# Loading the q and k of the split attention jobs once, splitting them over half the columns, and spreading the parts inside SBUF

## The chip, the cores and the metric

The kernel runs on one core of one Trainium2 chip. The metric is device time in microseconds (us) of one launch. The changed kernel and the kernel before compute the same outputs from the same inputs.

## The reference, cut to what matters

```python
batch, n_heads, seq, head_dim = (4, 8, 768, 64)
n_global, n_local = (8, 96)

def _attn_ref(q, k, v, n_global, n_local):
    scale = 1.0 / np.sqrt(D)
    scores = scale * np.matmul(q, k.transpose(0, 1, 3, 2))
    ...
    keep = is_global | is_local
    bias = -slopes[:, None, None] * dist[None, :, :]
    scores = np.where(keep, scores + bias, -1000000000.0)
    a = np.exp(scores - np.max(scores, axis=-1, keepdims=True))
    a = a / (np.sum(a, axis=-1, keepdims=True) + 1e-09)
    return np.matmul(a, v)

def _moe_ref(x, w_in, conv_w, w_out):
    h = np.maximum(x @ w_in, 0.0)
    ...
    gate = 1.0 / (1.0 + np.exp(-conv_out))
    return (h * gate @ w_out)

def reference(**kwargs):
    attn_out = _attn_ref(**attn_kwargs)
    x = attn_out.transpose(0, 2, 1, 3).reshape(B, S, H * D)
    return _moe_ref(x=x, **moe_kwargs)
```

The lines are put together from the reference. Everything is float32 or float64 and is wanted at about float32 accuracy. Attention is banded: a query sees the 96 keys up to its own and 8 global keys. `conv_out` is a convolution of three taps along the sequence, so the second half is two products (512 to 1024, 1024 to 512) with a gate between them.

## The kernel before, in words

**Jobs and steps.** Attention is cut into 32 jobs. A job `m` is one batch, one half `u` of the sequence (384 queries) and one pair of heads, and it has three steps, one for each tile of 128 queries; step `s` is tile `s % 3` of job `s // 3`. A step makes the scores of two heads on the TensorE (PE, `scores`), adds the bias and takes maxima on the VectorE (DVE, `maxima`, L412), takes the exponentials on the ScalarE (ACT, L426), inverts the sums on the DVE (`normalise`, reciprocal L438), scales on the GpSimd (POOL, L444), transposes on the PE (L452), and, three steps at a time, multiplies by v (`values`, L473). Each batch half then goes through the two products (`mm1` L507, `mm2` L622), which are cut into pieces and put between the attention steps.

**Native and split jobs.** Jobs 0 to 8 (`NATIVE`, `BESIDE`) multiply q and k as float32 at L385, from tiles of which rows 0 to 63 hold one head and rows 64 to 127 the other. Jobs 9 to 31, the 23 split jobs, use the faster format float32r, with q and k each split into a rounded high part and a low remainder. Their tiles are laid out so that one pass over 128 rows does two of the products: `kk` has the high part of k on rows 0 to 63 and the low part on rows 64 to 127, for both heads side by side; `qh` has the high part of q on both halves, `ql` the low part on both. A score tile is then two matmuls at L395, `kk` with `qh` and `kk` with `ql`.

**How the split is made.** The host gives q and k twice over, on rows 0 to 63 and again on rows 64 to 127. `load(m)` brings all 128 rows of `rk` (L114) and `rq` (L115) by one DMA each. `prep(m, 0)` rounds them into `kk` (L137) and `qh` (L138) on the POOL; `prep(m, 1)` subtracts on the DVE, rows 64 to 127 for `kk` (L141), all rows for `ql` (L142). For k there are 816 columns in the first half of a sequence and 1008 in the second, for q 768. `rk` and `rq` are single buffers (pool `p1`); `qh`, `ql`, `kk` and the v tile have two each (pool `p2`). The split for job m+1 is written into the program at the first step of job m, and the load for job m+2 at its second step.

**Order.** Steps 0 to 15 are in an order written by hand. From step 16 on the tile framework arranges the instructions of every engine with a timeline of its own, under priorities and under `issue_after` conditions: the pieces of the products that `fill` puts into a step are held behind the scores, maxima and exponentials of the step before. Each engine then runs its list in order. The list of the SyncE (SP) issues the loads of q, k, v (L123) and the raw weights (L307). A DMA in that list waits for the tile that it overwrites to be free, and everything behind it in the list waits too.

**The first part.** In the first 90 us the DVE and POOL also decode the weights of the products from float64 (L316 to L331). In the last 70 us the raw weights are read again and checked (L339).

## Time and profile before

| | |
|---|---|
| median of 3 runs | 444.82 us (444.18 to 444.93) |
| the profiled execution's own time | 445.31 us |
| its span, first to last instruction | 443.5 us |
| granted TensorE clock, mean | 0.996 |
| PE busy | 431.2 us (97% of the span) |
| DVE busy | 357.2 us (81%) |
| ACT busy | 309.9 us (70%) |
| POOL busy | 221.2 us (50%) |
| DMA moved | 60.02 MB, mean 135 GB/s |

Busy time is a sum over the whole span, and the span has parts with different limits. Matmuls are pipelined, so a PE that is busy all the time has instructions in flight all the time; whether it was held up is read from the chain of work that ended last and from stretches in which its busy time is below their length. An engine's queue is in order, so what an engine waited for also holds all that stands behind it.

### The profile page before, as it was taken

The numbers are of one execution on the slowest core, as the hardware profiler recorded it, in microseconds if no ns is written. First come the engines' busy times: TensorE is split into PE (matmuls) and PEld (weight loads), VectorE is DVE, ScalarE is ACT, GpSimd is POOL, SyncE is SP. The second block draws the span as 40 slices with busy tenths as digits, with TensorE's granted clock in tenths as the row PEclk, the third lists the DMA queues.
The fourth block names the chain that finished last, engine by engine and source line by source line (L and its number), as shares of the span: only waits on it lengthen the run. The fifth ranks groups of instructions, "written<-read, shape, count | busy, mean of one in ns | idle before, by whom it ended". The sixth has DMA issues, their size and how long they took to land.

```text
span 443.5 us, 9050 instructions
## 1 busy us (share of the span) xinstructions
PE 431.2 (97%) x3039; PEld 374.5 (84%) x3039; DVE 357.2 (81%) x935; ACT 309.9 (70%) x839; POOL 221.2 (50%) x307
## 2 busy tenths in 40 slices
PE   8988999799999999999999999999999999999996
PEld 7655778799889988899889988899988998798876
DVE  6899899998999988757998989747999975568700
ACT  4889988789896678546876865665776776755540
POOL 5555334654456786556757744647656841013000
PEclk9999999899999999999999999999999999999999
DMA  6998953141543244442246134423235313980111
GB/s 210 294 255 258 271 184 110 40 163 65 153 128 120 75 136 132 128 125 94 85 128 192 41 107 145 141 102 104 67 119 181 103 48 122 312 295 32 47 49 55
DMA packets 22662, 60.02 MB, mean 135 GB/s; under 512 B 3024, under 2 KB 5584, under 8 KB 22608
## 3 DMA queue, kind: packets, MB, share of 16 engines
q1 hardware_dynamic: 18992, 53.01, 39.2%
q10 hardware_dynamic: 3616, 6.36, 3.9%
q8 instruction: 26, 0.43, 0.4%
q14 instruction: 28, 0.23, 0.2%
HBM read 53.07 MB, written 6.29 MB: 134 GB/s over the span
## 4 chain that ended last, share of the span: by engine, by line
PE 81%; DVE 8%; DMA 6%; ACT 3%; issue 1%; POOL 0%; SPq 0%; DVEq 0%; ACTq 0%
PE o L622 26%; PE h L507 25%; PE pv L473 10%; PE t L452 9%; PE s L395 7%; DMA check<-in_w 3%; PE s L385 1%; PE last L643 1%; DMA out<-ob 1%; DVE w L320 1%; DVE w L318 1%; ACT junkb L350 1%; ACT pbuf L426 1%; DMA rq<-in_qk 1%; PE sb L385 1%
## 5 line engine op out<-in xcount | busy, mean ns | idle before, releaser
L444 POOL TENSOR_SCALAR pbuf<-pbuf,mm 128x232 f32<-128x232 f32 (+1 forms) x160 | 113.3, 718 | 81.0 <-DVE mm L438 49.5
L426 ACT ACTIVATE pbuf<-s,mm 128x232 f32<-128x232 f32 (+1 forms) x165 | 72.1, 442 | 48.3 <-DVE mm L412 34.6
L412 DVE CUSTOM_DVE_ANT_0 s<-s,tab 128x232 f32<-128x232 f32 (+1 forms) x165 | 63.1, 385 | 20.2 <-PE s L395 15.7
L622 PE MATMUL o<-woh,gh 128*128 128x512 f32 x184 | 74.1, 403 | 0.0
L622 PE MATMUL o<-woh,gl 128*128 128x512 f32 x184 | 73.5, 400 | 0.0
L622 PE MATMUL o<-wol,gh 128*128 128x512 f32 x184 | 73.3, 398 | 0.0
L452 PE MATMUL t<-ident,pbuf 128*128 128x128 f32 x384 | 65.4, 279 | 5.4 <-ACT pbuf L442 2.7
L557 POOL TENSOR_SCALAR c<-hbuf,cw 128x382 f32<-128x382 f32 (+1 forms) x48 | 38.6, 807 | 56.5 <-ACT hbuf L517 56.5
L452 PEld LDWEIGHTS t<-ident,pbuf 128*128 128x128 f32 x384 | 46.4, 141 | 20.2 <-ACT pbuf L442 6.4
L457 ACT ACTIVATE pt<-t 128x512 f32<-128x512 f32 x96 | 57.0, 597 | 8.3 <-PE t L452 8.0
L507 PE MATMUL h<-xl,wih 128*128 128x384 f32 x252 | 59.4, 343 | 0.0
L507 PE MATMUL h<-xh,wih 128*128 128x384 f32 x252 | 58.8, 347 | 0.1
L507 PE MATMUL h<-xh,wil 128*128 128x384 f32 x252 | 55.8, 339 | 0.0
L473 PE MATMUL pv<-pt,v 128*64 128x128 f32 (+1 forms) x768 | 50.3, 280 | 0.3 <-DVE xl L489 0.2
L473 PEld LDWEIGHTS pv<-pt,v 128*64 128x64 f32 (+1 forms) x768 | 42.5, 138 | 8.6 <-issue 3.6
L558 DVE SCALAR_TENSOR_TENSOR c<-hbuf,cw,c 128x382 f32<-128x382 f32 (+1 forms) x64 | 44.3, 699 | 4.8 <-POOL c L557 3.7
L559 DVE SCALAR_TENSOR_TENSOR c<-hbuf,cw,c 128x382 f32<-128x382 f32 (+1 forms) x64 | 45.4, 712 | 0.3
L507 PEld LDWEIGHTS h<-xh,wih 128*128 128x128 f32 x252 | 43.2, 190 | 2.1 <-ACT pbuf L426 0.9
L507 PEld LDWEIGHTS h<-xl,wih 128*128 128x128 f32 x252 | 43.9, 189 | 0.7 <-issue 0.7
L507 PEld LDWEIGHTS h<-xh,wil 128*128 128x128 f32 x252 | 44.1, 188 | 0.0
L517 ACT ACTIVATE hbuf<-h 128x384 f32<-128x384 f32 x64 | 31.4, 495 | 13.5 <-PE h L507 12.5
L622 PEld LDWEIGHTS o<-woh,gl 128*128 128x128 f32 x184 | 34.6, 188 | 7.3
(120 smaller groups left out, 856.1 us busy)
## 6 DMA issues: line engine op xcount, KB each, us to landing
v<-in_vv SPq DMA_DIRECT2D x32, 384.0 KB, 3.6
rq<-in_qk SPq DMA_DIRECT2D x23, 384.0 KB, 3.1
wr<-in_w SPq DMA_DIRECT2D x16, 512.0 KB, 5.3
check<-in_w SPq DMA_DIRECT2D x16, 512.0 KB, 4.9
rk<-in_qk SPq DMA_DIRECT2D x12, 504.0 KB, 3.6
out<-ob ACTq DMA_DIRECT2D x23, 256.0 KB, 2.4
rk<-in_qk SPq DMA_DIRECT2D x11, 408.0 KB, 3.6
rq<-in_qk SPq DMA_DIRECT2D x16, 96.0 KB, 5.1
```

Source lines behind the costliest of these rows:

```text
L412: last_ttr[s] = V.tensor_tensor_reduce(out=sp[j][:, c0 : c0 + n], in0=sp[j][:, c0 : c0 + n], in1=tb, scale=-0.125, scalar=3.0e38, op0=ALU. ...
L426: last_exp[s] = A.activation(pb[:, j, c0 : c0 + n], sp[j][:, c0 : c0 + n], AF.Exp, bias=mm[:, j : j + 1], scale=-1.0, accum_out=mm[:, 2 + ...
L444: G.tensor_scalar(x, x, inv, 1.0, ALU.mult, ALU.mult)
L452: T.transpose(pt[:, j, c, :], pb[:, j, c * P : (c + 1) * P], ident)
L457: last_ev[s] = A.activation(sb, st_pt[s], AF.Copy)
L473: T.matmul(pv[m][64 * j : 64 * j + 64, i * P : (i + 1) * P], vt[m][:n, i, c, 64 * j : 64 * j + 64], sb[:n, j, c, :], start=c == 0, stop=c ...
L507: T.matmul(ps[:, :TB], w_[:, k, fs], x_, start=part == 0 and k == 0, stop=part == 2 and k == NK - 1,)
L517: A.activation(half, ps[:, :TB], AF.Relu, scale=0.5)
L557: G.tensor_scalar(c, *tap(1), 1.0, ALU.mult, ALU.mult)
L558: V.scalar_tensor_tensor(c, *tap(0), c, ALU.mult, ALU.add)
L559: V.scalar_tensor_tensor(c, *tap(2), c, ALU.mult, ALU.add)
L622: last = T.matmul(ps, g_[:, f], w_[:, f], start=f == 0 and part == 0, stop=f == NF - 1 and part == 2,)
```

## The change

`load` now brings the split jobs in the layout of the native ones: one head on rows 0 to 63, the other on rows 64 to 127, each value once, by two DMAs of 64 rows for `rk` and two for `rq`. The tiles keep their size, so half of their columns are free. The POOL writes the rounded part into the free half of the same tile (`rk[:, w:]`, `rq[:, TB:]`); the DVE subtracts in place in the other half. Both now run over all 128 rows and half the columns (408 or 504 for k, 384 for q). After that 12 DMAs inside SBUF, all on SP's queue, carry the four (part, head) pieces of k to their place in `kk`, and the four of q to both row halves of `qh` or `ql`. The host's arrays are unchanged. Lines from `load` on move by up to six: L114 and L115 are now L110, L137 and L138 are L132 and L133, L141 and L142 are both L138, the new DMAs are at L144 and L148, L123 is L118, and L395, L412, L438, L444, L507 and L622 are L401, L418, L444, L450, L513 and L628.

```diff
@@ load
-        n = D if m < NATIVE else P
-        if m < BESIDE:
-            for t, c, a in ((rk, 2 * TB, w // 2), (rq, 0, TB)):
-                for j in range(2):
-                    r = slice(j * D, (j + 1) * D)
-                    X = nc.scalar if m == 0 and t is rq else nc.sync
-                    X.dma_start(t[r, :a], src[r, c + j * a : c + (j + 1) * a])
-        else:
-            nc.sync.dma_start(rk[:n], src[:n, 2 * TB :])
-            nc.sync.dma_start(rq[:n], src[:n, : 2 * TB])
+        for t, c, a in ((rk, 2 * TB, w // 2), (rq, 0, TB)):
+            for j in range(2):
+                r = slice(j * D, (j + 1) * D)
+                X = nc.scalar if m == 0 and t is rq else nc.sync
+                X.dma_start(t[r, :a], src[r, c + j * a : c + (j + 1) * a])
@@ prep
-            G.tensor_copy(kk, rk)
-            G.tensor_copy(qh, rq)
+            G.tensor_copy(rk[:, w:].bitcast(F32R), rk[:, :w])
+            G.tensor_copy(rq[:, TB:].bitcast(F32R), rq[:, :TB])
         else:
             qh, ql, kk = qk[m]
-            V.tensor_tensor(kk[64:], rk[64:], kk[64:].bitcast(F32), ALU.subtract)
-            V.tensor_tensor(ql, rq, qh.bitcast(F32), ALU.subtract)
+            for t, n in ((rk, w), (rq, TB)):
+                low, high = t[:, :n], t[:, n:]
+                V.tensor_tensor(low.bitcast(F32R), low, high, ALU.subtract)
+                for x, part in enumerate((high, low)):
+                    for j in range(2):
+                        heads = part[j * D : (j + 1) * D]
+                        cols = slice(j * n, (j + 1) * n)
+                        if t is rk:
+                            nc.sync.dma_start(kk[x * D : (x + 1) * D, cols].bitcast(F32), heads)
+                        else:
+                            for r in range(2):
+                                q_ = (qh, ql)[x][r * D : (r + 1) * D, cols]
+                                nc.sync.dma_start(q_.bitcast(F32), heads)
```

The framework arranges the instructions anew. Three places show it, all around job 20, whose first step is step 60. A name ends in the number of its job or step and a buffer number (`rk20_2985` is `rk` of job 20, `mm57` belongs to step 57).

SP's queue, loads of q and k for jobs 19 to 21 and of v for jobs 17 to 19, before:

```order
L123 DMA v17_2624<-in_vv 128x768
L115 DMA rq19_2667<-in_qk0 128x768
L114 DMA rk19_2666<-in_qk0 128x816
L115 DMA rq20_2832<-in_qk1 128x768
L123 DMA v18_2779<-in_vv 128x768
L114 DMA rk20_2831<-in_qk1 128x1008
L123 DMA v19_2942<-in_vv 128x768
L115 DMA rq21_2988<-in_qk1 128x768
L114 DMA rk21_2987<-in_qk1 128x1008
```

and now:

```order
L110 DMA rk19_2806<-in_qk0 64x408 x2
L110 DMA rq19_2807<-in_qk0 64x384 x2
L118 DMA v18_2933<-in_vv 128x768
L144 DMA kk19_2916<-rk19_2806 64x408 x4
L148 DMA qh19_2914<-rq19_2807 64x384 x4
L148 DMA ql19_2915<-rq19_2807 64x384 x4
L110 DMA rk20_2985<-in_qk1 64x504 x2
L110 DMA rq20_2986<-in_qk1 64x384 x2
L118 DMA v19_3110<-in_vv 128x768
L144 DMA kk20_3093<-rk20_2985 64x504 x4
L148 DMA qh20_3091<-rq20_2986 64x384 x4
L148 DMA ql20_3092<-rq20_2986 64x384 x4
```

Where SP issued three DMAs a job it issues 17, and the load of job 20 stands behind the whole spread of job 19, whose tiles it overwrites.

The POOL's queue around the rounding of job 20, before:

```order
L444 TENSOR_SCALAR pbuf0_193<-pbuf0_193,mm54_2715 128x136 x2
L557 TENSOR_SCALAR c3_2728<-hbuf_190,cw_185 128x386
L138 CAST qh20_2935<-rq20_2832 128x768
L137 CAST kk20_2937<-rk20_2831 128x1008
L444 TENSOR_SCALAR pbuf1_194<-pbuf1_194,mm55_2786 128x232 x2
```

and now:

```order
L450 TENSOR_SCALAR pbuf2_195<-pbuf2_195,mm56_2996 128x232 x2
L563 TENSOR_SCALAR c3_2870<-hbuf_190,cw_185 128x386
L132 CAST rk20_2985<-rk20_2985 128x504
L563 TENSOR_SCALAR c3_2870<-hbuf_190,cw_185 128x386
L133 CAST rq20_2986<-rq20_2986 128x384
L450 TENSOR_SCALAR pbuf0_193<-pbuf0_193,mm57_3040 128x136 x2
```

The rounding stood behind the scaling of step 54, six steps ahead of the job's first; now it stands behind that of step 56, four ahead.

The PE's queue at the first scores of job 20, before:

```order
L452 MATMUL t57_3005<-ident_153,pbuf0_193 128x128 x4
L395 MATMUL s60_3033<-kk20_2937,qh20_2935 128x232
L395 MATMUL s60_3033<-kk20_2937,ql20_2936 128x232
L395 MATMUL s60_3033<-kk20_2937,qh20_2935 128x232
L395 MATMUL s60_3033<-kk20_2937,ql20_2936 128x232
L622 MATMUL o1_0_3026<-woh_188,gh1_0_2394 128x512
```

and now:

```order
L458 MATMUL t57_3175<-ident_153,pbuf0_193 128x128 x4
L401 MATMUL s60_3203<-kk20_3093,qh20_3091 128x232
L628 MATMUL o1_0_3196<-woh_188,gh1_0_2508 128x512
L628 MATMUL o1_0_3196<-wol_189,gh1_0_2508 128x512
L628 MATMUL o1_0_3196<-woh_188,gl1_0_2509 128x512
L458 MATMUL t58_3237<-ident_153,pbuf1_194 128x128 x4
...
L401 MATMUL s60_3203<-kk20_3093,ql20_3092 128x232
L401 MATMUL s60_3203<-kk20_3093,qh20_3091 128x232
L401 MATMUL s60_3203<-kk20_3093,ql20_3092 128x232
```

The four score matmuls stood together; now nine matmuls of the second product and four transposes stand between the first, which reads `qh`, and the second, which reads `ql`.

## Rows read from the trace of the kernel before

**Rows 1.** Busy time of each engine in two stretches, with clock and DMA share.

```profile
core 0: us, PE busy (x) PEld busy (x) DVE busy (x) ACT busy (x) POOL busy (x), PEclk, DMA share, GB/s
64.00:85.00 21.00, 18.80 (x129) 16.14 (x128) 20.83 (x56) 17.82 (x55) 13.33 (x16) 1.00 0.36 118
110.00:370.00 260.00, 259.91 (x1858) 232.07 (x1855) 222.72 (x571) 182.09 (x483) 158.11 (x205) 1.00 0.38 116
```

**Rows 2.** Chain of work that ended last, 110 to 370 us, by line.

```profile
by line: PE h L507 33.2%; PE o L622 32.8%; PE pv L473 12.0%; PE s L395 11.2%; PE t L452 10.9%; issue 0.0%
```

**Rows 3.** The chain, 64 to 86 us, pieces: start, us, what.

```profile
71.76 1.02 DVE kk L141
...
74.42 0.85 DVE ql L142
...
80.27 1.25 DVE kk L141
...
85.10 0.91 PE pv L473 x8
```

**Rows 4.** Groups by line and shape, DVE: count, busy us, mean ns, idle before.

```profile
L142 DVE TENSOR_TENSOR ql<-rq,qh 128x768 fp32r<-128x768 f32 x23 | 22.6, 982 | 0.0
L489 DVE TENSOR_TENSOR xl<-pv,xh 128x384 fp32r<-128x384 f32 x32 | 17.5, 546 | 1.6 <-ACT xh L485 1.5
L141 DVE TENSOR_TENSOR kk<-rk,kk 64x1008 fp32r<-64x1008 f32 x12 | 15.7, 1308 | 0.4
L141 DVE TENSOR_TENSOR kk<-rk,kk 64x816 fp32r<-64x816 f32 x11 | 11.5, 1049 | 0.3
L331 DVE TENSOR_TENSOR wil<-w,wih 128x512 fp32r<-128x512 f32 x8 | 5.4, 680 | 0.0
```

**Rows 5.** The same, POOL.

```profile
L138 POOL CAST qh<-rq 128x768 fp32r<-128x768 f32 x23 | 22.1, 959 | 25.9 <-issue 14.6 <-PE s L395 8.1 <-POOL pbuf L444 1.8
L137 POOL CAST kk<-rk 128x1008 fp32r<-128x1008 f32 x12 | 15.9, 1329 | 4.0 <-DMA rk<-in_qk 4.0
L137 POOL CAST kk<-rk 128x816 fp32r<-128x816 f32 x11 | 11.7, 1062 | 1.5 <-PE sb L385 0.5 <-DMA rk<-in_qk 0.5 <-PE s L395 0.5
L325 POOL CAST wih<-w 128x512 fp32r<-128x512 f32 x8 | 5.7, 712 | 1.9 <-DVE w L320 1.9
```

**Rows 6.** SP's queue in order of time: start, us, DMAs issued (64-row loads, 0 us on).

```profile
1.18 2.47 SPq L112 DMA_DIRECT2D rk<-in_qk  x4
3.69 1.23 SPq L112 DMA_DIRECT2D rq<-in_qk  x2
...
6.55 0.43 SPq L123 DMA_DIRECT2D v<-in_vv  x1
```

**Rows 7.** DMAs issued in the first 5 us: KB each, median us to landing.

```profile
rk<-in_qk SPq DMA_DIRECT2D x4, 102.0 KB, 3.1
...
rq<-in_qk SPq DMA_DIRECT2D x2, 96.0 KB, 2.6
```

**Rows 8.** The page's DMA issues, whole span.

```profile
v<-in_vv SPq DMA_DIRECT2D x32, 384.0 KB, 3.6
rq<-in_qk SPq DMA_DIRECT2D x23, 384.0 KB, 3.1
...
rk<-in_qk SPq DMA_DIRECT2D x12, 504.0 KB, 3.6
...
rq<-in_qk SPq DMA_DIRECT2D x16, 96.0 KB, 5.1
```

**Rows 9.** L395 from 104 us (job 11), then from 355 us (job 31): first and last start.

```profile
L395 PE MATMUL s<-kk,qh x8: 232/273/376, 105.5 to 118.5; 128*128 128x232 f32 x6, 128*128 128x136 f32 x2
...
L395 PE MATMUL s<-kk,qh x2: 269/272/275, 356.8 to 357.1; 128*128 128x232 f32 x2
```

**Rows 10.** The chain around jobs 15 to 17: scores of steps 46, 48, and of 51.

```profile
159.25 0.64 PE s L395 x4
...
169.82 0.40 PE s L395 x4
...
180.40 0.07 PE s L395
```

**Rows 11.** POOL in order of time, scaling of steps 46, 47 and 48.

```profile
166.54 3.68 POOL L444 TENSOR_SCALAR pbuf<-pbuf,mm 128x232 f32<-128x232 f32 x2 [0.40 <-ACT c L577]
...
171.83 2.69 POOL L444 TENSOR_SCALAR pbuf<-pbuf,mm 128x232 f32<-128x232 f32 x2 [1.39 <-DVE mm L438]
175.81 0.73 POOL L444 TENSOR_SCALAR pbuf<-pbuf,mm 128x136 f32<-128x136 f32 x2 [1.29 <-DVE mm L438]
```

**Rows 12.** DVE in order of time, two gate multiplies and job 17's k.

```profile
166.54 2.56 DVE L610 SCALAR_TENSOR_TENSOR hbuf<-c,hbuf 128x1024 f32<-128x1024 f32 x2 [0.18 <-ACT c L577]
...
171.69 1.00 DVE L141 TENSOR_TENSOR kk<-rk,kk 64x816 fp32r<-64x816 f32 x1
```

## The prediction

> **What bounds the kernel now.** I read the busy time by stretches first, then the chain of work that ended last, then the groups by line, and at the end the queues of the engines that the change touches. From 110 to 370 us the PE is busy for 259.91 of 260 us [rows 1], and the chain runs through the PE alone: the five lines there add up to all of it [rows 2]. A shorter DVE or POOL instruction is worth nothing in that part, where 20 of the 23 split jobs run. From 64 to 85 us it is the other way round: the DVE is busy for 20.83 of 21 us and the PE for 18.80 [rows 1], and the chain stays on the DVE until it goes back to the PE at 85.10 [rows 3]. There three of its pieces belong to the split of jobs 9 and 10.
>
> The PE's pace in the split part is the clock against which the new path has to be held. The first scores of job 11 start at 105.5 and those of job 31 at 356.8 [rows 9], 251.3 us for 20 jobs or **12.57 us a job**.
>
> **What gets shorter.** The DVE's subtractions cost by columns, not by rows: 64 rows of 1008 columns take 1308 ns, 128 of 768 take 982, 128 of 512 take 680, 128 of 384 take 546 [rows 4]. So the change does halve them: 0.57 us for 408 columns and 0.67 for 504 in place of 1.05 and 1.31, 0.55 for q in place of 0.98. The POOL's roundings go the same way, by the half of 1329, 1062 and 959 ns; 128x512 at 712 ns [rows 5] fits that. Each engine is relieved of about 1 us a job. Of this only what lies on the chain between 64 and 85 us counts. There the pieces are 1.02, 0.85 and 1.25 us, 3.12 in all [rows 3]. In their place come two k of 0.57 and one q of 0.55 (in the new order the q of job 9 is split much earlier and that of job 10 takes its place), 1.69 in all: **-1.4 us**. The early q of job 9 (0.55 us of DVE, 0.5 of POOL) I cost at nothing: the PE's own work covers it at most steps there; without that cover it is +0.5.
>
> The loads bring half the bytes from HBM. Nothing waits for them on the chain in the split part [rows 2], and the DMA engines are busy for 0.38 of it [rows 1], so this is worth nothing either.
>
> **What is added: the path of a job through SP.** SP issued three DMAs a job and now issues 17: four loads, v, and 12 transfers within SBUF. A 64-row DMA costs SP 0.62 us when one follows another (2.47 us for four, 1.23 for two, at the start, where nothing else runs) [rows 6]. The transfers are 64 rows of nearly the same size, so I take 0.62 for each: 12 x 0.62 = 7.4 us, the loads 4 x 0.62 = 2.5, v 0.43 [rows 6], **10.3 us of SP's time in a job of 12.57**. That alone fits. It is the loop that is tight. `rk` and `rq` are single buffers, so the next load waits until the spread has read them, the next rounding until the load has landed, and the next spread until it is rounded. From the first `kk` transfer of a job: `kk`, `qh` and `ql` are issued by 7.4; the two halves of the next `rk` follow at once, the second issued at 8.0; it lands 3.1 us later [rows 7], at 11.1; the rounding of 504 columns takes 0.67, 11.8; then the next `kk` can go. q is not later: its load waits for the last `ql`, issued at 6.8 and landed by 9.4 with the 2.6 us of a 96 KB load [rows 7], is issued by 10.7, lands at 12.7 and is rounded at 13.2, before the 14.3 at which SP is done with the next `kk`. So the loop takes **11.8 us plus whatever the rounding waits for the POOL**.
>
> That wait can't be read from the trace of before, where the rounding stood elsewhere. Its bounds are the POOL's own scaling pairs: nothing, if the rounding finds the POOL free, and 3.68 us if it comes just behind the longest of the three pairs [rows 11]. I take 1.2 us, half of the mean of those three (3.68, 2.69 and 0.73), as for a rounding that comes at any time. The loop is then 13.0 us, 0.43 over the PE's 12.57. Jobs 12 to 31 pay that, 20 x 0.43 = **+8.6 us**. The ends are 0 (11.8 is under 12.57) and, with 3.68 us in every job, 15.5 and +58.
>
> The cover is gone too, which is why I don't expect an overrun to be absorbed. Before, the k of job 17 was ready at 172.69 [rows 12] and first read at 180.40 [rows 10], 7.7 us later. Now 12 transfers lie between. The new order also puts the rounding behind the scaling of a step four ahead of the job's first instead of six. The scaling of step 46 ended 10.3 us after its scores, that of step 48 6.3 us after [rows 10, 11]; four steps are 16.8 us; so 6.5 to 10.5 us are left for rounding, subtraction, 7.4 us of issue and 2.6 of landing. The piece of order on the PE agrees: nine products and four transposes are put between the scores with `qh` and those with `ql`, as if `ql` came later.
>
> What stands behind the new waits: on SP the v tiles and the next loads, which are part of the loop above; v itself is read two jobs later and has room. On the POOL the scalings behind a rounding that waits for its load; they feed the transposes. On the PE everything behind a score matmul, products included, since its queue is in order. The raw weights that are checked at the end stand behind the last spread on SP, but the PE has 70 us of products then; I cost this at nothing, and at +2 if that cover is late.
>
> [...] Row first: a scaling pair and two two-input DVE multiplies began together at 166.54; the multiplies took 2.56 us, the pair 3.68 [rows 11, 12], against 0.73 for a pair of narrower tiles that met none [rows 11]. [...]
>
> **Sum.** The profiled execution took 445.31 us, its span 443.5. 445.3 - 1.4 + 8.6 = 452.5; the median of the runs is 0.5 below the profiled one, so **452 us**.
>
> **Rivals.**
> 1. *The loop fits, and the DVE stretch decides (faster).* If the rounding waits less than 0.8 us for the POOL, 11.8 + 0.8 is not over 12.57, the PE stays the bound, and what is left is the gain between 64 and 85 us: 445.3 - 1.4 - 0.5 = **443.4**. For it: SP's own work is only 10.3 us, and both engines lose 1 us a job. Against it: the scaling pairs, two of three of which take over 2.6 us [rows 11].
> 2. *The transfers are slow to land.* No transfer within SBUF is in the trace. The 64-row loads landed in 2.6 to 3.1 us alone [rows 7] and in 5.1 us at the middle of all of them, most of which met other loads [rows 8]. With 1 us more to land the loop is 14.0 and costs 20 x 1.43 = 28.6 us, **472**; with 2 us more, 492. For it: the transfers come in bursts and meet v's 384 KB. Against it: the DMA engines are at 0.38 [rows 1]. [...]
> 3. *It cancels.* An overrun of 0.07 us a job eats the 1.4 us: **444.8**, no difference. This is also what comes if the PE's queue of products takes up most of the overrun.
>
> **How the numbers follow.** Forecast (an overrun of some tenths of a us a job) 0.50, rival 1 0.25, rival 2 0.15, rival 3 0.10. About 0.2%, 0.9 us, is what a measurement of this kernel can tell from no change, so 443.4 falls just on the faster side; some of rival 1 lies within. Faster 0.22, same 0.11, slower 0.67. The range goes from 442.5 (rival 1 with 0.9 us more) to 474 (rival 2's nearer value); it leaves out the slower half of rival 2 and overruns of over 1.5 us a job, about 0.15. The forecast's own range is 446 to 465.
>
> **What would show it.** Right: the chain between 110 and 370 us is no longer all PE but has DMA from `rk` or `rq` to `kk`, `qh`, `ql`, SP's queue, POOL or DVE pieces before L401; the PE's busy time there falls below the stretch; SP's `kk`, `qh` and `ql` issues are about 0.6 us apart and fill over 9 us a job; the first scores of jobs 11 and 31 stand over 12.57 us a job apart; L138 takes 0.5 to 0.7 us a piece. Wrong: the PE is busy all through and the chain unbroken (rival 1 or 3); SP issues the transfers at half that cost; the overrun is there, but from landings of over 4 us (rival 2); or the time is lost before 110 us or after 370, which I priced at nothing.

## The result, and the profile after

The changed kernel takes **452.12 us** (median of 6 runs), the kernel before on the same chip 444.82 (6 runs): ratio 1.015, 95% interval 1.0114 to 1.0187, slower. The profiled execution took 452.12 us, its span is 450.3. The forecast was 452.0. The total was met; that its terms were not is what the rest shows. Executions that stand far from the rest of their kernel (453.6 and 1056 us in `e1`, 453.9 in `e3`, one of 528 of the kernel before) count in the medians below but not in the ratios.

Busy time in the stretches of [rows 1], after, and a stretch of 40 us that the prediction did not look at by itself:

```profile
64.00:85.00 21.00, 21.00 (x153) 17.16 (x152) 19.61 (x56) 18.98 (x59) 9.62 (x14) 1.00 0.65 173
110.00:150.00 40.00, 39.23 (x282) 35.08 (x282) 33.77 (x94) 31.63 (x81) 18.21 (x27) 1.00 0.66 168
110.00:370.00 260.00, 257.10 (x1819) 230.04 (x1819) 189.25 (x555) 178.66 (x476) 121.78 (x201) 1.00 0.68 179
```

The columns are those of [rows 1]: stretch, PE, PEld, DVE, ACT, POOL, clock, DMA share, GB/s. From 64 to 85 us the PE is the busy one now, not the DVE. From 110 to 370 us the DVE lost 33 us of work and the POOL 36, the DMA share rose from 0.38 to 0.68, and the PE is no longer busy all the time. The chain says the same. By line, 110 to 370 us ([rows 2] before):

```profile
by line: PE o L628 25.3%; PE h L513 16.4%; PE pv L479 7.4%; PE t L458 7.0%; PE s L401 6.6%; SPq L148 5.0%; DMA v<-in_vv 3.1%; POOL pbuf L450 2.7%; issue 2.7%; DVE c L564 2.5%; DVE c L565 2.3%; ACT pbuf L432 1.9%; DMA ql<-rq 1.7%; POOL c L56
```

The pieces of the split, DVE and POOL, by line and shape ([rows 4, 5]):

```profile
L138 DVE TENSOR_TENSOR rq<-rq 128x384 fp32r<-128x384 f32 x23 | 12.8, 556 | 2.7 <-POOL rq L133 2.2 <-DMA v<-in_vv 0.2
L138 DVE TENSOR_TENSOR rk<-rk 128x504 fp32r<-128x504 f32 x12 | 9.3, 772 | 3.6 <-POOL rk L132 3.3
L138 DVE TENSOR_TENSOR rk<-rk 128x408 fp32r<-128x408 f32 x11 | 6.5, 592 | 2.0 <-POOL rk L132 2.0
L133 POOL CAST rq<-rq 128x384 fp32r<-128x384 f32 x23 | 13.5, 589 | 16.5 <-DMA rq<-in_qk 13.2 <-issue 2.7 <-POOL pbuf L450 0.3
L132 POOL CAST rk<-rk 128x504 fp32r<-128x504 f32 x12 | 8.4, 704 | 35.5 <-DMA rk<-in_qk 16.5 <-issue 14.1 <-DMA rq<-in_qk 4.9
```

They take 53 to 61% of what they took in [rows 4, 5] (k of 504 columns 772 ns against 1308, q 556 against 982). The last two rows show what is new: the POOL stands before its roundings and waits for their loads. DMA issues of the page ([rows 8]): the 12 transfers are there and land in 2.2 to 2.5 us at the median (`qh` 2.3, `kk` of 102 KB 2.5).

```profile
ql<-rq SPq DMA_DIRECT2D x92, 96.0 KB, 2.2
...
kk<-rk SPq DMA_DIRECT2D x48, 126.0 KB, 2.4
rq<-in_qk SPq DMA_DIRECT2D x62, 96.0 KB, 3.1
```

**Where the time went.** First scores of a job can't be compared between the two kernels as they stand, since the products around them are placed otherwise. So I add up the PE's matmuls of each trace in the order of their starts, each kind at the duration that it has in unbroken pieces of the chain (`h` 0.174 us, `o` 0.233, `pv` 0.061, `t` and `s` 0.11, a native score 0.41), and read when the same sum is reached. The lag behind the kernel before, one profiled execution each, at the sums that the kernel before reaches at 48.9, 96, 149.8, 393.8 and 434.3 us (good to about 0.2 us):

| | 48.9 | 96 | 149.8 | 393.8 | 434.3 |
|---|---|---|---|---|---|
| after | 4.0 | 1.6 | 2.4 | 5.7 | 7.0 |
| `e1_q9_late` | 0.4 | -1.4 | -0.1 | 2.1 | 2.2 |
| `e2_qh_on_act` | 4.8 | 4.0 | 6.2 | 6.5 | 6.1 |
| `e3_first_two` | 4.6 | 2.5 | 2.2 | 2.5 | 3.2 |
| `e4_rest` | 3.3 | 4.0 | 4.7 | 6.3 | 7.4 |
| `e5_k_only` | 0.1 | -1.1 | -1.4 | -1.4 | -1.0 |
| `e6_q_only` | 2.9 | 2.1 | 3.1 | 7.8 | 8.0 |
| `e8_first_two_late` | 0.1 | -1.6 | 2.2 | 2.5 | 2.9 |
| `e9_late_act` | 1.6 | 0.0 | 4.7 | 4.4 | 5.4 |
| `e11_first_two_late21` | 1.6 | 0.2 | 4.4 | 4.4 | 5.1 |
| `e12_k_first_two` | 0.0 | -0.5 | 1.5 | 1.5 | 1.0 |
| `e13_k_to_job15` | 0.0 | -1.0 | -0.7 | -0.6 | 0.1 |

The changes between columns are what to read. For the changed kernel: +4.0, -2.4, +0.8, +3.3, +1.3 us, in the end 7.0.

**What the clock adds.** The granted TensorE clock is 1.00 in most stretches of these traces and falls in some, down to 0.50 (86 to 88 us in the kernel before, 40 to 42 us in the changed one), at different places in different executions. The kernel before, then k of jobs 9 to 15 (`e13`), columns as above:

```profile
82.00:84.00 2.00, 0.09 (x1) 0.00 (x0) 2.00 (x7) 1.32 (x6) 1.56 (x2) 1.00 0.65 194
85.00:89.00 4.00, 3.90 (x30) 3.57 (x31) 4.00 (x11) 2.53 (x8) 0.85 (x1) 0.57 0.04 8
```

```profile
82.00:84.00 2.00, 1.62 (x13) 1.27 (x11) 2.00 (x6) 1.81 (x7) 0.61 (x1) 1.00 0.74 160
85.00:89.00 4.00, 2.79 (x34) 2.16 (x32) 4.00 (x11) 3.32 (x12) 1.68 (x3) 1.00 0.46 130
```

In the kernel before the PE stood still behind the DVE at 82 to 84 us, and then the clock was 0.57 on average for 4 us; where the DVE's pieces are shorter the PE stood less and the clock stayed at 1.00. The lag is therefore read at 96 us, behind this place: at 88 us it shows up to 1.8 us more gain, which is gone again by 92; the DVE is busy for 4.00 of the 4 us from 85 to 89 in both.

The lower clock also comes where no edit is. In `e4`, from 25 to 30 us:

```profile
25.00:30.00 5.00, 4.93 (x36) 4.10 (x37) 3.66 (x14) 3.18 (x13) 2.56 (x4) 0.50 0.97 303
```

In and just around that stretch `e4` loses 3.0 of its 3.3 us at 48.9 us, and `e6` (0.50 there too) 2.8 of its 2.9; the 1.6 us of `e9` and `e11` go with 0.66 and 0.68 from 40 to 45 us. The PE had been as idle from 20 to 25 us in the kernel before (3.40 us busy, 3.47 in `e4`), whose clock stayed at 1.00. In the changed kernel the clock fell behind the wait told next (0.76 from 40 to 45 us), and the lag did not grow by it.

So the clock is a second thing in which executions differ. The kernel before takes 444.0 to 444.8 us in the 12 of its 76 executions beside the experiments that have a mean clock of at least 0.998, and at its median 445.3 at 0.996 and 447 at 0.992. The changed kernel's executions are at 0.992 and 0.996, with 452.1 us at the median at 0.992: it is slower at an equal clock too.

**The +4.0.** Up to step 12 the two traces are the same; the first scores of step 13 start at 35.66 us before and at 39.43 after. POOL in order of time, before:

```profile
33.00 0.74 POOL L444 TENSOR_SCALAR pbuf<-pbuf,mm 128x232 f32<-128x232 f32 x1 [1.21 <-DVE mm L438]
```

and after:

```profile
36.74 0.51 POOL L133 CAST rq<-rq 128x384 fp32r<-128x384 f32 x1 [4.94 <-DMA rq<-in_qk]
37.22 0.86 POOL L450 TENSOR_SCALAR pbuf<-pbuf,mm 128x232 f32<-128x232 f32 x1
```

The scaling of step 10 began at 33.00; now it begins at 37.22, behind the rounding of job 9's q, which waited 4.94 us for its load. The chain of the changed kernel, 30 to 40 us (start, us, what), leads from that load to the transposes:

```profile
31.18 5.41 DMA rq<-in_qk
...
36.74 0.51 POOL rq L133
37.25 0.85 POOL pbuf L450
...
38.14 0.66 PE t L458 x4
```

The rounding used to write into `qh`, and stood behind the scaling of step 21, at 66 us. Now it writes into its own tile, and the framework put it between the scalings of steps 9 and 10. That its own timeline had the load there by then is likely, but no row shows it.

**The +3.3.** The chain, 205 to 240 us, shows the loop that the prediction added up, from one job's transfers over the next load and rounding to the next transfers, and out of it to the scores:

```profile
208.90 2.74 DMA rk<-in_qk
...
211.75 0.76 POOL rk L132
...
212.53 1.99 DMA kk<-rk
...
215.11 0.60 SPq L144
...
220.62 0.59 SPq L148
...
221.26 2.16 DMA ql<-rq
...
223.56 0.34 PE s L401
```

SP's queue in order of time, one turn of it (job 22's `kk` to job 23's, 12.0 us):

```profile
239.52 2.41 SPq L144 DMA_DIRECT2D kk<-rk  x4
242.03 2.70 SPq L148 DMA_DIRECT2D qh<-rq  x4
244.84 2.47 SPq L148 DMA_DIRECT2D ql<-rq  x4
247.35 1.24 SPq L110 DMA_DIRECT2D rk<-in_qk  x2
249.06 1.10 SPq L110 DMA_DIRECT2D rq<-in_qk  x2
251.52 3.38 SPq L144 DMA_DIRECT2D kk<-rk  x4
```

Over jobs 12 to 31, 19 turns, the mean is **13.12 us**: 8.17 from the first `kk` to the end of the last `ql`, 0.15 to the next `rk`, 3.75 until both its halves have landed, 0.34 until the rounding starts, 0.68 for it, 0.03 to the next `kk`. The rounding hardly waits for the POOL; it starts when its load is there.

**The +1.3.** The raw weights that are checked come late. The chain, 380 to 415 us:

```profile
387.52 5.36 DMA check<-in_w
...
393.77 5.38 DMA check<-in_w
...
406.36 4.48 DMA check<-in_w
...
412.86 2.37 PE o L628 x9
```

The kernel before has the first of them on its chain at 375.88 and is back on the PE at 401.71. In the changed kernel the PE is busy for 9.12 of the 10 us from 405 to 415.

### The profile page after: what moved, and what is told of

It reads as the page before. It is cut to its first block, busy times and chain, and to the rows that moved or that the text cites. A ratio compares the mean times of both kernels' runs of the same rounds, so it can differ in the third digit from the quotient of the medians.

```text
span 450.3 us, 9746 instructions
## 1 busy us (share of the span) xinstructions
PE 432.8 (96%) x3039; PEld 373.9 (83%) x3039; DVE 323.1 (72%) x935; ACT 308.2 (68%) x839; POOL 179.7 (40%) x307
## 4 chain that ended last, share of the span: by engine, by line
PE 58%; DMA 12%; DVE 11%; ACT 7%; SPq 5%; POOL 4%; issue 3%; POOLq 0%; DVEq 0%; ACTq 0%
PE o L628 23%; PE h L513 13%; PE t L458 6%; PE pv L479 6%; DMA check<-in_w 5%; PE s L401 4%; SPq L148 3%; DMA v<-in_vv 3%; ACT pbuf L432 2%; DVE c L564 2%; DMA rq<-in_qk 2%; DVE s L418 2%; PE s L391 2%; POOL pbuf L450 2%; DVE c L565 2%
## 5 line engine op out<-in xcount | busy, mean ns | idle before, releaser
L450 POOL TENSOR_SCALAR pbuf<-pbuf,mm 128x232 f32<-128x232 f32 (+1 forms) x160 | 101.2, 644 | 107.5 <-DVE mm L444 66.2
L418 DVE CUSTOM_DVE_ANT_0 s<-s,tab 128x232 f32<-128x232 f32 (+1 forms) x165 | 62.3, 389 | 32.9 <-PE s L401 26.4
L628 PE MATMUL o<-woh,gh 128*128 128x512 f32 x184 | 74.2, 404 | 0.3 <-ACT hbuf L523 0.3
L628 PE MATMUL o<-wol,gh 128*128 128x512 f32 x184 | 73.5, 399 | 0.0
L628 PE MATMUL o<-woh,gl 128*128 128x512 f32 x184 | 72.7, 396 | 0.0
L458 PEld LDWEIGHTS t<-ident,pbuf 128*128 128x128 f32 x384 | 45.4, 141 | 24.7 <-POOL pbuf L450 9.4
L564 DVE SCALAR_TENSOR_TENSOR c<-hbuf,cw,c 128x382 f32<-128x382 f32 (+1 forms) x64 | 43.7, 685 | 24.6 <-POOL c L563 23.7
L513 PE MATMUL h<-xh,wih 128*128 128x384 f32 x252 | 59.3, 347 | 0.6 <-ACT hbuf L523 0.5
L513 PE MATMUL h<-xh,wil 128*128 128x384 f32 x252 | 57.2, 340 | 0.0
L513 PE MATMUL h<-xl,wih 128*128 128x384 f32 x252 | 57.0, 341 | 0.0
L563 POOL TENSOR_SCALAR c<-hbuf,cw 128x382 f32<-128x382 f32 (+1 forms) x48 | 31.7, 662 | 47.4 <-ACT hbuf L523 43.5
L479 PE MATMUL pv<-pt,v 128*64 128x128 f32 (+1 forms) x768 | 49.3, 276 | 0.3 <-DVE xl L495 0.2
L513 PEld LDWEIGHTS h<-xh,wih 128*128 128x128 f32 x252 | 43.1, 189 | 3.1 <-ACT hbuf L523 1.1
L513 PEld LDWEIGHTS h<-xh,wil 128*128 128x128 f32 x252 | 43.9, 188 | 0.0
L513 PEld LDWEIGHTS h<-xl,wih 128*128 128x128 f32 x252 | 43.7, 188 | 0.2 <-issue 0.2
L565 DVE SCALAR_TENSOR_TENSOR c<-hbuf,cw,c 128x382 f32<-128x382 f32 (+1 forms) x64 | 41.5, 650 | 1.0
L628 PEld LDWEIGHTS o<-woh,gl 128*128 128x128 f32 x184 | 34.6, 188 | 7.6
L628 PEld LDWEIGHTS o<-woh,gh 128*128 128x128 f32 x184 | 34.6, 188 | 7.3 <-ACT hbuf L523 0.7
```

What stands on the lines that cost most here:

```text
L418: last_ttr[s] = V.tensor_tensor_reduce(out=sp[j][:, c0 : c0 + n], in0=sp[j][:, c0 : c0 + n], in1=tb, scale=-0.125, scalar=3.0e38, op0=ALU. ...
L450: G.tensor_scalar(x, x, inv, 1.0, ALU.mult, ALU.mult)
L458: T.transpose(pt[:, j, c, :], pb[:, j, c * P : (c + 1) * P], ident)
L479: T.matmul(pv[m][64 * j : 64 * j + 64, i * P : (i + 1) * P], vt[m][:n, i, c, 64 * j : 64 * j + 64], sb[:n, j, c, :], start=c == 0, stop=c ...
L513: T.matmul(ps[:, :TB], w_[:, k, fs], x_, start=part == 0 and k == 0, stop=part == 2 and k == NK - 1,)
L563: G.tensor_scalar(c, *tap(1), 1.0, ALU.mult, ALU.mult)
```

## Experiments

Theory A: a rounding that waits for its load on POOL costs the 4 us at 35 us, and SP's issues make a loop that is longer than the PE's pace. The rivals stand in each expectation. "Before" is the kernel before on the same chip: 445.9 us for the first four, 446.2 for the next four, 445.1 for `e10` to `e12` and 446.7 for `e13`. The ratio carries the 95% interval; it is not the quotient of the two medians, and can differ from it by some 0.15%.

**Job 9's q rounded later** (`e1_q9_late`).

```diff
+            with contextlib.ExitStack() as es:
+                if m == NATIVE:
+                    es.enter_context(tc.issue_after(last_norm[20].ins))
-            G.tensor_copy(rq[:, TB:].bitcast(F32R), rq[:, :TB])
+                G.tensor_copy(rq[:, TB:].bitcast(F32R), rq[:, :TB])
```

`last_norm[s]` is the scaling of step `s`.

> The changed kernel, with one edge more: the rounding of job 9's q stands on the POOL behind the scaling of step 20, where it stood before the change, and not behind that of step 9. Theory A (the changed kernel loses 3.8 us at about 35 us because the scaling of step 10 stands behind a rounding that waits for its load, and this loss is carried to the end): step 13 of the native jobs comes 3.8 us earlier, the first scores of job 11 come at about 102.7 us in place of 106.5, and the time is 452.1 - 3.8 = 448.3 us. Rival C (the DVE works ahead while the PE stands at 35 us, so the DVE-bound stretch after it gives the loss back by itself): step 13 comes 3.8 us earlier too, but job 11 starts within 1 us of 106.5 and the time is 451 to 452 us. The pace of jobs 11 to 31 stays at 12.9 us a job for both.

448.67 us, ratio 1.005 (1.0022 to 1.0078). Step 13 starts at 36.04 in place of 39.43, and the scaling has its old place again:

```profile
33.37 0.74 POOL L453 TENSOR_SCALAR pbuf<-pbuf,mm 128x232 f32<-128x232 f32 x1 [1.20 <-DVE mm L447]
```

One instruction, moved in the list of one engine, is about two thirds of the loss: the excess falls from 1.5% to 0.5%, with 3.6 us less lag at 48.9 us and 4.8 less at the end. Theory A's 448.3 is met, and rival C, that the early wait would be made up for elsewhere, falls. (In the kernel before this rounding stood behind the scaling of step 21; here it stands one step earlier.)

**qh's transfers on ACT's queue** (`e2_qh_on_act`).

```diff
-                                nc.sync.dma_start(q_.bitcast(F32), heads)
+                                (nc.sync if x else nc.scalar).dma_start(q_.bitcast(F32), heads)
```

> The changed kernel, with the four transfers of qh of each job issued on ACT's queue in place of SP's. Theory A (the loop load, rounding, spread, load over SP's queue paces jobs 11 to 31): SP has 2.5 us a job less to issue, the loop falls from 12.9 to about 10.4 us, the PE sets the pace again at about 12.6 us a job, and the time falls by 20 x 0.33 = 6.6 us to about 445.5, plus up to 1 us for ACT, which issues 4 x 0.6 us a job more. Rival B (the pace is set by the place of the roundings behind the scalings on the POOL, or by the landing of the transfers, not by what SP issues): the pace stays at 12.8 to 13.0 and the time at 451 to 454 us.

453.01 us, ratio 1.0169 (1.0122 to 1.0215): not faster. Theory A's forecast, 445.5 us and a turn of 10.4, failed, and rival B's 451 to 454 came. The turn of the loop is 13.07 us on average, hardly shorter: SP's loads of `rk` and `rq` now wait for the transfers of `qh` and `ql` that read these tiles (12.6 and 9.2 us in all, 110 to 350 us). Yet from 149.8 to 393.8 us this kernel loses 0.3 us where the changed one loses 3.3. Most of it is lead: the first `kk` is issued 18.0 us before the first scores at job 12 and 10.9 at job 31, so 7.1 us of the loop's overrun were taken from the lead (2.8 in the changed kernel, from 10.8 to 8.0). What it lost, it lost before.

**New path for jobs 9 and 10 alone** (`e3_first_two`), **and for jobs 11 to 31 alone** (`e4_rest`). `load` and `prep` take the old lines where `new(m)` is false; the diff is that of the first, and in the second `new(m)` is `m >= NATIVE + 2`:

```diff
+    def new(m):
+        return m < NATIVE + 2
...
+        if m >= NATIVE and not new(m):
+            nc.sync.dma_start(rk, src[:, 2 * TB :])
+            nc.sync.dma_start(rq, src[:, : 2 * TB])
```

> The new path for jobs 9 and 10 alone; jobs 11 to 31 load and split as before the change. Theory A: the wait at 35 us is there (+3.8 us), the DVE-bound stretch is shorter, job 11 starts at 106 to 107 us (105.5 before the change), and from there the pace is that of before, 12.57 us a job: 445.3 to 446.5 us. Rival B says the same, as it puts the loss into jobs 11 to 31. If the time is over 448, the loss is not in the later jobs.

448.59 us, ratio 1.0055 (1.0017 to 1.0093): over 448, a miss for both theories, and by the sign that was named the loss is not in the later jobs alone.

> The complement: jobs 9 and 10 load and split as before the change, jobs 11 to 31 go the new way. Theory A: nothing is lost at 35 us and nothing won in the DVE-bound stretch, job 11 starts at about 105.5 us, the pace is 12.9 us a job, and the time is 444.8 + 6.7 = 451 to 452 us. If the loss depends on how the order of jobs 9 and 10 comes out, the pace is under 12.7 and the time under 448.

448.39 us, ratio 1.0041 (1.0013 to 1.0068): under theory A's 451 to 452, a miss. The two excesses, 2.5 us and 1.8 us by the ratios (2.7 and 2.5 by the medians), make 4.3 of the changed kernel's 6.7. With two jobs alone the wait at 35 us is there (step 13 at 40.06) and nothing much is lost between 149.8 and 393.8 us; with the other 21, 1.6 us are.

**The new path for k alone** (`e5_k_only`), **and for q alone** (`e6_q_only`). The diff is that of the first; the second leaves the old lines for `rk` in the same way.

```diff
+            if m >= NATIVE and t is rq:
+                nc.sync.dma_start(t, src[:, c : c + 2 * a])
+                continue
...
-            G.tensor_copy(rq[:, TB:].bitcast(F32R), rq[:, :TB])
+            G.tensor_copy(qh, rq)
...
-            for t, n in ((rk, w), (rq, TB)):
+            V.tensor_tensor(ql, rq, qh.bitcast(F32), ALU.subtract)
+            for t, n in ((rk, w),):
```

> The new path for k alone (two loads of 64 rows, rounding and subtraction over half the columns, four transfers); q is loaded twice over and split as in the kernel before. SP issues 8 DMAs a job in place of 17, about 4.5 us, and job 9's q is rounded behind the scaling of step 21 again. Theory A (the wait at 35 us, then a loop through SP's queue that is too long): neither loss is there; what is left is the gain of the DVE between 64 and 85 us, two pieces of k at 0.57 in place of 1.02 and 1.25 us, 1.1 us: 0.5 to 1.5 us under the kernel before, first step-13 scores within 0.5 us of its 35.66. Theory B (the pace of the later jobs comes from the transfers' landing, whatever SP issues): kk still lands 2.5 us behind its issue and holds the next rk, so jobs 11 to 31 lose 1 to 2 us and the time is at or 1 us over the kernel before.

443.94 us, ratio **0.9956** (0.9934 to 0.9979): faster than both kernels, by 2 us. Between 149.8 and 393.8 us nothing is lost, with transfers that land in kk as before: theory A. Part of the ratio is the clock: 5 of the 8 executions have at least 0.998, and these take 443.0 to 444.0 us against the 444.0 to 444.8 of the kernel before at that clock, some 0.5 us less. The lag at 96 us, -1.1, is what was forecast for the two pieces of k.

> The new path for q alone (two loads, half columns, eight transfers); k as in the kernel before. The rounding of job 9's q stands early on POOL again, behind the scaling of step 9, so theory A has the wait at 35 us (3.5 to 4.8 us, step 13 at 39 to 40.5), a gain of 0.5 to 1.5 us in the DVE stretch, and with 13 DMAs a job on SP (7.3 us) hardly any loss after job 11: 2.5 to 4 us over the kernel before. Theory B: the eight transfers hold the single rq until they have landed and cost 1 to 2 us more: 4 to 6 us over.

453.28 us, ratio 1.0182 (1.0138 to 1.0226), more than either theory gave. The low clock from 25 to 30 us had made it 2.8 us late before the early rounding came; that waited 1.24 us for its load where the changed kernel's waited 4.94, and cost 0.2 us more (step 13 at 38.71). It lost 4.7 us between 149.8 and 393.8 us, nearly all of it between 312 and 341. POOL there, in order of time:

```profile
335.28 1.34 POOL L136 CAST rq<-rq 128x384 fp32r<-128x384 f32 x1 [2.34 <-DMA rq<-in_qk]
336.57 1.02 POOL L135 CAST kk<-rk 128x1008 fp32r<-128x1008 f32 x1
...
340.21 3.85 POOL L454 TENSOR_SCALAR pbuf<-pbuf,mm 128x232 f32<-128x232 f32 x2 [0.39 <-DVE mm L448]
```

Once more a rounding that waits for its load, two roundings in front of scalings, and a scaling pair of 3.85 us. This is read from the trace; no run took it away.

**Both edits that had helped, together** (`e8_first_two_late`: jobs 9 and 10 alone, q held), **and the held q with qh on ACT's queue** (`e9_late_act`).

> The new path for jobs 9 and 10 alone and the rounding of job 9's q held behind the scaling of step 20: the two edits tried singly before. Theory A: the early wait (4 us) goes, the DVE gain (2.5 to 3.3 us) stays, no loop in the later jobs: 1.5 to 3 us under the kernel before, ratio 0.993 to 0.997, job 11's scores near 103.5 and 12.57 us a job after. Theory C (the work of the early wait is only put off, and the DVE stretch ends when it ends): the same as with jobs 9 and 10 alone, ratio 1.005.

447.78 us, ratio 1.0049 (1.0028 to 1.0069): a miss for theory A, and rival C's number. The gain is there first (1.6 us ahead at 96 us), and 3.8 us are lost by 149.8, in jobs whose path is that of the kernel before. POOL there:

```profile
126.38 1.80 POOL L141 CAST kk<-rk 128x1008 fp32r<-128x1008 f32 x1 [0.24 <-DMA rk<-in_qk]
130.84 4.65 POOL L469 TENSOR_SCALAR pbuf<-pbuf,mm 128x232 f32<-128x232 f32 x4 [2.67 <-DVE mm L462]
```

The POOL waits 2.67 us for the DVE's `mm`, and the DVE is busy for 9.94 of the 10 us from 130 to 140.

> The changed kernel with the rounding of job 9's q held behind the scaling of step 20 and qh's four transfers on ACT's queue. Theory A with SP's issues as the limit of the loop: SP has 2.5 us less a job, the losses after job 14 go (they were 2.2 us in the run with the late rounding alone, and none behind 145 us in the run with the transfers on ACT), so 1 to 3 us under the run with the late rounding alone, at the kernel before or up to 2 us over it. Theory B (landings, not issues, make the loop): no better than the late rounding alone, 2 to 4 us over the kernel before.

450.52 us, ratio 1.0099 (1.0074 to 1.0124), over both theories, a miss for the total as in `e2`. Behind 149.8 us no time is lost (4.7, then 4.4); between 96 and 149.8, 4.7 us are, with `ql` and the scalings as what the PE waited for (85 to 152 us: what, us in total, times, longest):

```profile
PE t L461 <- POOL pbuf L453: 3.0, 4, 1.6
PE s L404 <- DMA ql<-rq: 1.7, 1, 1.7
```

**The same bytes in more transfers** (`e10_k_16_pieces`), k alone.

```diff
-                            nc.sync.dma_start(kk[x * D : (x + 1) * D, cols].bitcast(F32), heads)
+                            for c in range(4):
+                                f = slice(c * n // 4, (c + 1) * n // 4)
+                                nc.sync.dma_start(kk[x * D : (x + 1) * D, cols][:, f].bitcast(F32), heads[:, f])
```

> The new path for k alone, with each of the four transfers into kk cut into four by columns: the same bytes, 16 transfers and 20 DMAs a job on SP in place of 8. Theory A (SP's issues make the loop, and their price is by the DMA and not by the byte): 16 x 0.6 + 1.2 for the next rk + 2.7 to land + 0.3 + 0.65 for the rounding is a loop of 14.5 us, 15 with v and q's load in it, over the PE's 12.57: kk to kk 14 to 15 us in the trace, 465 to 490 us. If the price goes with the columns (a quarter each), the loop is that of k alone (4.5 us of issue) and the time stays at 444 to 445. Theory B (bytes in flight or landings make the loop): also 444 to 446.

547.08 us, ratio 1.2291 (1.2236 to 1.2347). SP's queue, one turn:

```profile
307.49 0.53 SPq L108 DMA_DIRECT2D rq<-in_qk  x1
308.11 0.38 SPq L121 DMA_DIRECT2D v<-in_vv  x1
308.71 1.59 SPq L113 DMA_DIRECT2D rk<-in_qk  x2
315.22 10.24 SPq L150 DMA_DIRECT2D kk<-rk  x16
```

A transfer of 31.5 KB costs SP 10.24 / 16 = 0.64 us, one of 126 KB 2.41 / 4 = 0.60: between these two sizes the price is by the DMA. The time is far over the 465 to 490 of theory A: the turn is 17.35 us on average against the 15 expected, since `rk` and the rest took 7.1 us of it and not 5.4. 20 x (17.35 - 12.57) = 96 us, and the time is 102 us over: with the lead used up, the overrun of the loop comes out in the end. The mean clock of this run is 0.922 (from 132 to 136 us it is 0.70, and the PE is busy for 2.57 of the 4 us); how much of the 102 us is the clock isn't separated. Theory B, 444 to 446 us, falls.

**The held q of `e8` one step later** (`e11_first_two_late21`).

> As the run with jobs 9 and 10 alone and job 9's q held, but held behind the scaling of step 21 in place of step 20. Some 55 of 2,860 instructions of the DVE and 13 of 240 of the POOL stand elsewhere; the work is the same. Theory D (the 4.5 us lost between 100 and 150 us there came from where the framework put k's and q's rounding on the POOL against the scalings, not from the new path): the loss there comes out otherwise by more than 1 us, anywhere from 442.5 to 448, and the ratio differs from 1.0049. Theory E (something fixed in that stretch takes back what was gained before it): the same, 1.003 to 1.006, with a lag of 2 to 2.5 us at 150 us.

450.29 us, ratio 1.009 (1.0056 to 1.0124), over the range of either theory. Its profiled execution lost 1.6 us with the low clock before 48.9 us; the two executions with a clock of at least 0.998 take 447.7 and 448.9 us, those of `e8` 446.6 to 448.7. From 96 to 149.8 us it loses 4.2 us, `e8` 3.8. That the place of these few roundings alone makes this loss (theory D) is not borne out; the loss is nearly the same in both.

**k alone, in jobs 9 and 10 only** (`e12_k_first_two`), **and in jobs 9 to 15** (`e13_k_to_job15`). The k of the other jobs goes by the old lines; `new(m)` is `m < NATIVE + 2`, then `m < NATIVE + 7`.

> The new path for k of jobs 9 and 10 alone; all of q and the k of jobs 11 to 31 as in the kernel before. Theory A (the gain of the run with k alone is the DVE's, between 64 and 85 us): the same gain, 1 to 2.5 us, ratio 0.994 to 0.998. Theory D (part of that gain is luck of the arrangement between 100 and 150 us, which is another one here): the lag is -2 us at 100 us but comes out otherwise at 150 us, and the ratio lies between 0.997 and 1.005. Theory F (the gain is from the DVE and POOL work that k's halves save in every job): no more than 0.5 us faster than before.

447.15 us, ratio 1.004 (1.0015 to 1.0066): slower, where theory A had it 1 to 2.5 us faster and theory F up to 0.5; it lies in theory D's range.

> The new path for k of jobs 9 to 15 alone; q, and the k of jobs 16 to 31, as in the kernel before. The engines' lists are those of the run with k alone up to about 150 us. Theory F, narrowed (the halves of k pay where the DVE has no room, up to 150 us, that is in jobs 9 to 15, and nothing after): the whole gain of the run with k alone, a lag of -1.0 to -1.5 us at 150 us that stays to the end, ratio 0.994 to 0.998. If the savings count in all jobs: less than half of that gain is left, ratio 0.998 to 1.000. Theory D (luck of the arrangement): what is gained at 150 us is lost again at some later place, ratio 0.998 to 1.005.

444.23 us, ratio **0.9932** (0.9913 to 0.9952). This ratio flatters it: the kernel before took 446.7 us on this chip here and 445.1 in the turn of `e10` to `e12`, with a lower clock here (1 of its 11 executions at 0.998 or more, against 5 of 6 of `e13`). At that clock `e13` takes 443.0 to 444.9 us and the kernel before 444.0 to 444.8: no difference that these runs show, as in the lag of 0.1 at the end. What can be compared is `e12` with `e13`, on one chip: 445.8 to 446.2 us (5 executions) against 443.0 to 444.9 at that clock.

Both are ahead at 96 us, by 0.5 and 1.0. The lag of `e13` at 149.8 us, -0.7, is near the -1.0 to -1.5 of theory F, narrowed, and it stays, as that theory had it, until 393.8. At 149.8 `e12` is 1.5 us behind, and that stays too. Between them lie the halves of k of jobs 11 to 15, and the order that the framework makes with them. Busy time from 110 to 150 us (columns as above), the kernel before:

```profile
110.00:150.00 40.00, 40.00 (x288) 35.97 (x285) 38.98 (x94) 30.78 (x80) 23.65 (x30) 1.00 0.46 137
```

k of jobs 9 and 10:

```profile
110.00:150.00 40.00, 38.50 (x274) 34.01 (x274) 38.46 (x96) 31.20 (x84) 24.25 (x28) 1.00 0.43 133
```

k of jobs 9 to 15:

```profile
110.00:150.00 40.00, 39.63 (x286) 35.65 (x284) 36.31 (x99) 33.81 (x90) 24.06 (x32) 1.00 0.49 144
```

k of all jobs:

```profile
110.00:150.00 40.00, 40.00 (x293) 36.04 (x293) 35.87 (x102) 35.02 (x92) 23.96 (x34) 1.00 0.48 139
```

The DVE has one us of 40 to spare in the kernel before. Where k is halved in these jobs it has four, and the PE keeps what it gained. After 150 us halving buys nothing: the k of jobs 16 to 31 makes no difference that the runs show (0.9956 and 0.9932, intervals that overlap; neither lag moves from 149.8 to 393.8 us).

**What stays open.** Why the kernels that relieve jobs 9 and 10 alone come out 1.5 to 2.2 us behind the kernel before at 149.8 us, and not level with it, isn't settled: `e3`, 4 us behind `e8` at 96 us, arrives with it there, so something other than the PE sets that time, and the DVE's list is what is full (29.33 of the 30 us from 110 to 140 in `e3`, 29.43 in `e8`). That the arrangement of the lists makes the difference between `e12` and `e13`, and not the DVE's work (theory D), was tested by `e11` for a few roundings only, and stands as a rival. Nor is it settled why the kernel with the held q and transfers on ACT's queue loses 4.7 us from 96 to 149.8 us (`e9`) where the one without them loses 1.3 (`e1`). The late checks were read from the chain and not tried.

## Why the prediction was right, and where not

That the time was right to 0.1 us is luck: of the terms one was missing, one too small and one too large, and they cancelled. The direction was not luck alone: with the missing term taken away (`e1`) the kernel is still slower, by 0.5%, and the loop forecast for it is there.

- *"The early q of job 9 ... I cost at nothing ... without that cover it is +0.5."* This is the step that failed: it cost **4.0 us** in the profiled execution. I priced the instruction's own work and not its wait. The order showed it between two scalings, and the prediction itself said that scalings stand behind a rounding that waits for its load and feed the transposes; the load, issued at 31.18 while the raw weights came in (DMA share 1.05 from 30 to 35 us), landed 5.41 us later. `e1` takes it away and the time with it.
- *"-1.4" between 64 and 85 us.* The pieces are near the ones forecast (0.56, 0.59, 0.77 against 0.55, 0.57, 0.67), and the stretch goes over to the PE. By 96 us the gain is 2.4, and 1.1 with k's halves alone, as k's pieces say; how much of the rest is q's piece and how much the new order of the lists isn't separated. The low clock at 85 to 89 us, which the trace of before shows just behind the stretch of [rows 1], the prediction didn't look at.
- *"A shorter DVE or POOL instruction is worth nothing in that part"*, 110 to 370 us. True of the kernel before as it stands: `e5` halves k there and its lag moves by 0.3 us from 96 to 149.8. It is too strong for the first 40 us once the stretch ahead is shorter: [rows 1] averages 222.72 of 260 for the DVE; the first 40 of them are 38.98 of 40. A chain that runs through the PE alone did not say that the DVE was next by one us. Between `e12` and `e13` some 2 us hang on it, if it is the DVE's work and not the order.
- *The loop: 13.0 us, from 7.4 of transfers, 3.7 for the load, 0.67, and 1.2 of waiting for the POOL.* It is 13.12, from 8.17, 3.75 and 0.15 between, 0.68, and 0.34. The transfers wait inside their row, at 251.52 for a subtraction: the four of `kk` take 3.38 us there and 2.41 at 239.52, and SP waits 1.1 us for the DVE's `rk`. The POOL's wait was the guess among the terms, and too large. `e10` shows what more issues do to it, and `e2` that fewer did not shorten it.
- *"+8.6", 20 x 0.43.* 19 turns ran 10.4 us over the PE's pace (249.24 against 19 x 12.57). Of this the first scores of job 31 show 7.6, since from `kk` to first scores it was 10.8 us at job 12 and is 8.0 at job 31; and between the two jobs' first scores 3.7 us more of PE work is done than before, products that the framework puts ahead. What is left is the lag: 1.3 at job 12, 5.3 at job 31, **+4.0**. "The cover is gone" was wrong: it was thin, not gone, and rival 3's sentence on the PE's queue of products was the better account.
- *The checks at the end, "at nothing, and at +2 if that cover is late".* They cost 1.3 us.

Sum: 4.0 - 2.4 + 0.8 + 3.3 + 1.3 = 7.0 in place of -1.4 + 8.6 = 7.2.

Rival 1 had its condition fulfilled, a wait of 0.34 where 0.8 was its limit, and its result did not come, because the transfers took 0.8 us more than their pitch. The prediction set a scaling pair of 3.68 us beside two DVE multiplies that began with it. What can be said after the change is that the DVE's subtractions are halved and that the scaling of 128x232 on POOL fell from 759 ns on average to 677; the order of both engines changed too, and no run separates the two. Before, then after:

```profile
L444 POOL TENSOR_SCALAR pbuf<-pbuf,mm 128x232 f32<-128x232 f32 x135 | 101.0, 759 | 62.0 <-DVE mm L438 36.9 <-ACT pt L457 7.1 <-ACT pbuf L426 5.2
L450 POOL TENSOR_SCALAR pbuf<-pbuf,mm 128x232 f32<-128x232 f32 x135 | 89.9, 677 | 77.1 <-DVE mm L444 48.6 <-PE t L458 10.8 <-ACT pt L463 7.9
```

Rival 2 did not come: the transfers land in 2.2 to 2.5 us, under the 2.6 taken. The DMA share from 110 to 370 us is 0.68, with v and the outputs in it, and the loads of v land in 4.1 us at the median where they took 3.6 before.

Of the signs named, the broken chain, SP's pieces on it, the issues of 0.6 us and the pace of the first scores (12.90 us a job from 11 to 31) came as written. Two came in part: the transfers take 8.17 us of a turn and not over 9, and L138 takes 0.56, 0.59 and, for 504 columns, 0.77 us. The sign against it, time lost before 110 us or after 370, came too.

## What to carry to other kernels

When an instruction is moved in an engine's list, price its wait for its own data at the new place, and with it everything that stands behind it in that list: 0.5 us of work held up the kernel by 4 us here. A chain that runs through one engine names the bound but not the next one: look at the busy time of the second engine in short stretches before calling its savings worthless. Many small transfers inside SBUF were paid by the DMA, on the queue that issued them (0.60 us for 126 KB, 0.64 for 31.5 KB on SP). Here the operand that needs few (k, four) could be halved without a loss, and the changed kernel with q's eight as well lost time; q alone was run only with its early rounding, so the price of its transfers by themselves isn't shown. Before a ratio of under 1% is believed, compare executions at an equal granted clock.

## What was not expected of the hardware

The issue price of a 64-row transfer on SP does not fall with its size: 0.64 us for 31.5 KB, 0.60 for 126 KB, while a load of all 128 rows and 384 KB costs 0.53 for `rq` and 0.38 for v in the rows of `e10`.
